# Decode attention and GLU block: four heads of one batch in a group, K in two halves of 32 KB rows, V as one tile of 64 KB rows

## The chip, the cores and the metric

One core of a Trainium2 chip. The experiments ran on three chips, each group beside runs of the kernel before on its own chip; the ratios are taken there. The metric is the device time of the kernel in microseconds (us), the median of several runs. "PE" is TensorE, "DVE" VectorE, "ACT" ScalarE, "POOL" GpSimd; "the transfer engines" are the core's 16 DMA engines.

A ratio is the mean time of one kernel's runs over the mean of the other's of the same rounds, so it is not quite the ratio of the medians that are quoted.

## The reference, cut to what matters

```python
# B=2, one query token, D=512, 32 heads of Dh=128, 8192 cached keys
q = (layernorm(x) @ wq)                                   # [2, 32, 128]
scores = einsum("bhqd,bhkd->bhqk", q, k_cache) * Dh**-0.5 # K: 134 MB
o = einsum("bhqk,bhkd->bhqd", softmax(scores), v_cache)   # V: 134 MB
h = x + o.reshape(2, 1, 4096) @ wo                        # wo: 4.2 MB
out = h + W_down(relu(gate(ln(h))) * up(ln(h)))           # F=1376, 4.2 MB
```

Every byte of K and V is read once: 268 of the 281 MB that the kernel reads.

## The kernel before

One unit of work is a pair of heads of one batch: 64 partitions for each head, 128 keys in each partition, so that a row is 128 x 128 x 2 bytes = 32 KB, for K and for V. Four slots of 4 MB hold K and V of two pairs in turn. The sync engine issues all loads.

```python
def kv(cache, p):
    hp, b = divmod(p, B)
    return cache[b, 2 * hp:2 * hp + 2].rearrange("h (p j) d -> (h p) (j d)", p=64)
def load(s, cache, p):
    nc.sync.dma_start(slot[s][:], kv(cache, p)).then_inc(slot_sem[s], 16)
```

DVE computes the scores of 96 of the 128 keys (a multiply with q, four halving adds and a reduction), PE those of the other 32 (transposes and matmuls). ACT takes the exponentials, one instruction per head and part; PE multiplies them with V. The loop over two pairs is a hardware loop on PE, DVE and ACT; POOL, SP and the tail are unrolled.

```python
with nc.Fori(0, NI, ...):                    # PE
    k_part(body, 0, ...)
    collect(body, 6)
    pv(body, 0, ...)
    k_part(body, 1, ...)
    o_gather(body)                           # the former outputs into one accumulator
    pv(body, 1, ...)
...
v_loads = [p] if p < NP - 5 else ...         # SP: slot of V is reloaded when its PV is done
for r in v_loads:
    sp.wait(tokp("pv", r))
    if r < NP - 3:
        load((2 * r + 1) % 4, A_v_cache, r + 2)
```

The whole text follows.

The softmax here doesn't subtract the row's maximum and nothing guards it: scores larger than these inputs give would overflow.

Of the kernel before, what the change touches and what calls it, by code (L numbers as in the profile page):

```python
# [39 lines left out]
def bass_sequential_preLN__gqa_block_cached__glu_gated_reglu__decode_kernel(  # L40
# [28 lines left out]
    DR = (H - 2) * Dh // 128  # L69
    NM = 6  # L70
# [5 lines left out]
    with ExitStack() as es:  # L76
# [14 lines left out]
        slot_sem = [S(f"slot{i}") for i in range(4)]  # L91
# [9 lines left out]
        slot = [sb(f"slot{i}", [128, SLOT], BF16) for i in range(4)]  # L101
        X = sb("X", [128, DR * D], BF16)
        wo_last = sb("wo_last", [128, 2 * D], BF16)
# [3 lines left out]
        QW = 8 + Dh  # L107
        q_all = sb("q_all", [128, NP, QW], BF16)
        qT = sb("qT", [128, NP * 2], BF16)
        q_c = [sb(f"q_c{i}", [128, QW], BF16) for i in range(2)]  # L110
# [5 lines left out]
        wo_rows, q_row = scr[:, 0:2 * D], scr[:, 2 * D:4 * D]  # L116
        pick = scr[:, 4 * D:5 * D].rearrange("p (s n) -> p s n", n=64)
        place = scr[:, 5 * D:6 * D].rearrange("p (h r d) -> p h r d", h=2, r=2)
# [9 lines left out]
        zs = sb("zs", [128, 4, 2], F32)  # L128
        zr = sb("zr", [128, 4], F32)
        zi = sb("zi", [128, 4], F32)  # L130
        O_cur = sb("O_cur", [128, 4], BF16)
        O_l = sb("O_l", [128, 2, B, 128], BF16)
        O_all = sb("O_all", [128, DR, B], BF16)
        mask = sb("mask", [128, DR // 2, NM], BF16)
        rows = sb("rows", [128, 2 * DR], BF16)
        rsel = sb("rsel", [128, 2, DR], BF16)
# [13 lines left out]
        zero = O_l[:, 0, 0, 0:B * DR]  # L150
# [8 lines left out]
        def kv(cache, p):  # L159
            hp, b = divmod(p, B)  # L160
            return cache[b, 2 * hp:2 * hp + 2].rearrange("h (p j) d -> (h p) (j d)", p=64)

        def tile(s):
            return slot[s][:].rearrange("p (j d) -> p j d", d=Dh)

        if True:

            def program():

                def load(s, cache, p):  # L170
                    nc.sync.dma_start(slot[s][:], kv(cache, p)).then_inc(slot_sem[s], 16)  # L171

                nc.scalar.dma_start(x_row, A_x[:, 0]).then_inc(sem_x, 16)
                nc.sync.dma_start(slot[3][:], A_wq.rearrange("(p c) n -> p (c n)", c=DC)).then_inc(sem_wq, 16)  # L174
                nc.sync.dma_start(  # L175
                    wo_rows, A_wo[128 * DR:].rearrange("(p r) n -> p (r n)", r=2)).then_inc(sem_wl, 16)
                load(0, A_k_cache, 0)
                load(1, A_v_cache, 0)
                load(2, A_k_cache, 1)


# [7 lines left out]
                for c in range(4):  # L189
                    pool.last()  # L190
                    pool.run(nc.gpsimd.tensor_copy(
                        out=sel[32 * c:32 * c + 32, :].rearrange("p (j q a) -> p j q a", j=VJ, q=PG),
                        in_=ident_f[32 * c:32 * c + 32, 32 * c:32 * c + 16].rearrange("p (q j a) -> p j q a", j=VJ, q=PG)))
# [6 lines left out]
                for sgn, base in ((1, 0), (-1, DR - 1)):  # L200
                    pool.last()
                    pool.run(nc.gpsimd.affine_select(
                        out=mask[:], in_=mask[:], pattern=[[2 * sgn, DR // 2], [-DR * sgn, NM]],
                        compare_op=ALU.is_ge, fill=0.0, base=base, channel_multiplier=sgn))
# [3 lines left out]
                for bank in Op:  # L208
# [4 lines left out]
                    in_=ident[:].rearrange("p (t r) -> p t r", r=32)[:, :, 0:B].unsqueeze(3).broadcast_to([128, 4, B, 64])))  # L213
                pool.run(nc.gpsimd.memset(place, 0.0))
                pool.last()
                for r in range(2):
                    t_place = pool.run(nc.gpsimd.tensor_copy(
                        out=place[:, :, r, r:128:2], in_=ident[:].rearrange("p (h i) -> p h i", h=2)))
# [31 lines left out]
                wq = slot[3][:].rearrange("p (c n) -> p c n", c=DC)  # L250
# [16 lines left out]
                for m in range(8):  # L267
# [5 lines left out]
                    out=qT[:].rearrange("p (t m b a) -> p t m b a", t=4, b=B, a=2),  # L273
                    in_=Wp[:].bitcast(BF16).rearrange("p (m a t r) -> p t m r a", m=4, a=2, t=4)[:, :, :, 0:B, :]))
                pe.wait(t_qT)
                for r in range(2):
                    for h in range(2):
                        i = nc.tensor.matmul(
                            Sp[r][64 * h:64 * h + 64, 0:2 * NP], lhsT=ident[:].rearrange("p (n r) -> p r n", r=2)[:, r, :],
                            rhs=qT[:], start=True, stop=True)  # L280
                t = pe.run(i)
                dve.run(nc.vector.memset(q_all[:, :, 0:8], 0.0))
                dve.wait(t)
                dve.last()
                for r in range(2):
                    for h in range(2):
                        t_q2 = dve.run(nc.vector.tensor_copy(
                            out=q_all[64 * h:64 * h + 64, :, 4 * r + 2 * h:4 * r + 2 * h + 2],
                            in_=Sp[r][64 * h:64 * h + 64, 0:2 * NP].rearrange("p (n a) -> p n a", a=2)))
# [8 lines left out]
                t_sel = dve.run(nc.vector.tensor_copy(out=rows[:, DR:], in_=rows[:, 0:DR]))  # L298
                sp.wait(t_q)
                load(3, A_v_cache, 1)  # L300
# [6 lines left out]
                for m in range(8):  # L307
                    if m >= 2:
                        pe.wait(t_cp[m - 2])
                    for a in range(2):  # L310
                        mm = nc.tensor.matmul(
                            Op[m % 2][64 * a:64 * a + 64, :], lhsT=pick[:, m, :],
                            rhs=q_row.rearrange("p (m a d) -> p m a d", a=2, d=Dh)[:, :, a, :], start=True, stop=True)
                    t_mm[m] = pe.run(mm)
                    act.wait(t_mm[m])
                    p0 = 8 * (m // B) + m % B
                    t_cp[m] = act.run(nc.scalar.activation(
                        out=q_all[:, p0:p0 + 7:2, 8:QW], in_=Op[m % 2][:].rearrange("p (k d) -> p k d", d=Dh),
                        func=ACT.Copy))
                t_q_b = t_cp[7]  # L320
                pe.wait((sem_wl, 16))
                for h in range(2):
                    for r in range(2):
                        mm = nc.tensor.matmul(
                            Tp[h][:], lhsT=place[:, h, r, :], rhs=wo_rows[:, r * D:(r + 1) * D], start=(r == 0), stop=(r == 1))
                    t = pe.run(mm)
                    act.wait(t)
                    t_wl = act.run(nc.scalar.activation(out=wo_last[:, h * D:(h + 1) * D], in_=Tp[h][:], func=ACT.Copy))
# [7 lines left out]
                nc.tensor.matmul(Ob[:, 0:ZC + 8], lhsT=onesn[:], rhs=ident[:, 0:ZC + 8], start=True, stop=True)  # L336
# [14 lines left out]
                def k_part(T, p, ev, k_wait):  # L351
                    s = (2 * p) % 4
                    k_t = tile(s)
# [3 lines left out]
                    def score(g):  # L357
                        wait(a2p, ev[g])
                        kv_ = kT[g % 2][:].rearrange("p (k n r) -> p k r n", n=128, r=2)
                        for k in range(GT // 2):  # L360
                            jj = g * GT + 2 * k
                            for r in range(2):
                                i = nc.tensor.matmul(  # L363
                                    Sp[p % 2][:, 2 * jj:2 * jj + 4], lhsT=kv_[:, k, r, :],
                                    rhs=q_c[p % 2][:, 4 * r:4 * r + 4], start=(r == 0), stop=(r == 1))
# [25 lines left out]
                def pv(T, p, parts, between=None):  # L391
                    s = (2 * p + 1) % 4
                    v_t = tile(s)
                    q = p % PG
                    n = 0
                    for j0, j1, waits in parts:
# [5 lines left out]
                        for j in range(j0, j1, VJ):  # L402
# [5 lines left out]
                            if T is body and n == 0:  # L408
# [4 lines left out]
                def collect(T, a):  # L413
                    nc.tensor.wait_ge(a2p, a)
                    for jj in range(VJ):
                        i = nc.tensor.matmul(  # L416
                            Ob[:, 0:4], lhsT=os_sb[:, jj * Dh:(jj + 1) * Dh],
                            rhs=sel[:, 4 * jj:4 * jj + 4], start=(jj == 0), stop=(jj == VJ - 1))
# [5 lines left out]
                def z_sum(bank):  # L424
                    return nc.tensor.matmul(bank[:, ZC:ZC + 8], lhsT=ones_f[:], rhs=zs[:], start=True, stop=True)  # L425

                def o_gather(T):
                    for a in range(2):
                        for b in range(B):
                            i = nc.tensor.matmul(  # L430
                                Op[1][:, b * DR:(b + 1) * DR], lhsT=O_l[:, a, b, :], rhs=rsel[:, a, :],
                                start=False, stop=False, skip_group_check=True)
                    T.mark("og", i)

                with nc.Fori(0, NI, engines=OrderedEngineSet([nc.tensor.engine])):
                    k_part(body, 0, (1, 2, 3, 4), ((k2p, 1),))
                    collect(body, 6)
                    pv(body, 0, ((JC, J, ((slot_sem[1], 16), (a2p, 5))), (0, JC, ((a2p, 7),))))
                    k_part(body, 1, (8, 9, 10, 11), ((k2p, 2),))
                    nc.tensor.wait_ge(l2p, 1)  # L440
                    o_gather(body)
                    nc.tensor.sem_inc(l2p, -1)
                    pv(body, 1, ((JC, J, ((slot_sem[3], 16), (a2p, 12))), (0, JC, ((a2p, EV),))))
                    z_sum(Ob)
                    nc.tensor.sem_inc(slot_sem[1], -16)
                    nc.tensor.sem_inc(slot_sem[3], -16)
# [11 lines left out]
                nc.tensor.wait_ge(l2p, 1)  # L458
                o_gather(tail)
# [7 lines left out]
                pv(tail, P0, ((JC, J, ((slot_sem[1], 16),)), (0, JC, ((a2p, 13),))))  # L467
# [14 lines left out]
                def tokp(kind, p, *g):  # L482
                    return tok(kind if kind == "og" else (kind, p) + g, p // 2)
# [5 lines left out]
                def exp(p, k, src):  # L489
                    q = p % PG  # L490
                    j0, j1 = ((JC, J), (0, JC))[k]
                    for a in range(2):
                        h = slice(64 * a, 64 * a + 64)
                        i = nc.scalar.activation(  # L494
                            out=e_t[q][h, j0 // VJ:j1 // VJ, 8 * q:8 * q + 8].rearrange(
                                "p g (j a) -> p g j a", a=2)[:, :, :, a],
                            in_=src(h, a), func=ACT.Exp, scale=inv_sqrt_dh,
                            accum_out=zs[h, 2 * q + a, k:k + 1])
# [357 lines left out]
```

## Time and profile before

| | before |
|---|---|
| time, median | 659.99 us (659.79 to 660.20, 6 runs) |
| span of the profiled run | 658.6 us |
| bytes read | 281.05 MB, 427 GB/s over the span |
| transfer packets | 10645 |
| DVE, PE, ACT, POOL busy | 469, 326, 214, 73 us |
| one turn of the loop (two K and two V loads) | 38.86 us |

How to read it: the profile counts an engine as busy while an instruction of it runs. No computing engine is near the span, and the row of slices for the transfer engines is full from end to end (0.9 or more in each of the 40 but the first and the last). The turn is the time from one multiply that waits for K to the next such multiply, in the chain that ended last: twelve turns between 131.15 and 597.46 us. The lines are in the prediction below.

### The profile page before, as it was taken

What the parts mean: (1) busy time and instruction counts of PE and PEld (TensorE: products, weight loads), DVE (VectorE), ACT (ScalarE), POOL (GpSimd) and SP (SyncE); (2) the same over time, 40 slices, a digit from 0 to 9 for tenths busy, and PEclk for the clock granted to TensorE, in tenths of its full rate; (3) what the DMA queues carried; (4) which work ended last, traced back from release to release, by engine and by line L of the source; (5) the groups of instructions that cost most, each with busy time, mean ns of one, the idle gap of its engine ahead of it and who ended that gap; (6) DMA issues with size and microseconds to landing.
All of it is one profiled execution on the core that took longest, in us unless ns stands there. A gap on an engine that the chain in (4) does not pass through costs nothing.

```text
span 658.6 us, 7569 instructions
## 1 busy us (share of the span) xinstructions
PE 326.1 (50%) x3066; PEld 192.1 (29%) x3067; DVE 469.4 (71%) x280; ACT 214.2 (33%) x433; POOL 72.7 (11%) x125
## 2 busy tenths in 40 slices
PE   2753444435554354644535453554445454454586
PEld 0431322214332132422213232322323222232354
DVE  1585576788767678776768867677876767787991
ACT  1622332243342233334223243323324322433151
POOL 3001002020200202020020201102020010202000
PEclk9999565565576555576655577555566755557567
DMA  8999999999999999999999999999999999999997
GB/s 366 445 426 437 426 442 418 442 420 444 424 436 438 422 440 420 444 422 438 430 432 438 422 440 420 444 422 438 440 422 436 424 438 424 440 428 436 434 415 307
DMA packets 10645, 281.17 MB, mean 427 GB/s; under 512 B 1190, under 2 KB 1292, under 8 KB 1804
## 3 DMA queue, kind: packets, MB, share of 16 engines
q1 hardware_dynamic: 10628, 281.06, 99.4%
q8 instruction: 5, 0.08, 0.0%
q14 instruction: 4, 0.03, 0.0%
q10 hardware_dynamic: 8, 0.00, 0.0%
HBM read 281.05 MB, written 0.00 MB: 427 GB/s over the span
## 4 chain that ended last, share of the span: by engine, by line
DMA 80%; DVE 18%; issue 1%; SPq 0%; DVEq 0%; PE 0%
DMA slot<-in_A_k_cache_dram 76%; DVE prod L539 16%; DMA slot<-in_B_W_down_dram 4%; DVE prod L548 2%; DVE scores L553 0%; SPq L171 0%; SPq L702 0%; SPq L698 0%; DVE kT L815 0%; DVEq L586 0%; PE O L807 0%; DVEq L590 0%; SPq L175 0%; SPq L174 0%; DVE zi L505 0%
## 5 line engine op out<-in xcount | busy, mean ns | idle before, releaser
L539 DVE TENSOR_TENSOR prod<-slot,q_c 128x12288 bf16<-128x12288 bf16 x32 | 209.9, 6558 | 148.1 <-DMA slot<-in_A_k_cache_dram 141.4
L404 PE MATMUL O<-slot,e 128*16 128x512 bf16 x1024 | 117.2, 609 | 219.3 <-ACT e L494 146.3
L548 DVE TENSOR_TENSOR prod<-prod 128x6144 bf16<-128x6144 bf16 (+3 forms) x128 | 212.3, 1658 | 7.8
L565 ACT ACTIVATE kT<-T 128x1024 bf16<-128x1024 bf16 x128 | 126.2, 1022 | 144.6 <-PE T L380 141.7
L380 PE MATMUL T<-ident_f,slot 128*128 128x128 f32 x512 | 112.8, 376 | 29.4 <-DVEq L586 29.4
L404 PEld LDWEIGHTS O<-slot,e 128*16 128x16 bf16 x1024 | 26.1, 112 | 284.6 <-ACT e L494 172.9
L494 ACT ACTIVATE e<-scores 64x96 bf16<-64x96 f32 x64 | 19.5, 304 | 239.8 <-DVEq L600 237.0
L380 PEld LDWEIGHTS T<-ident_f,slot 128*128 128x128 f32 x512 | 81.9, 193 | 44.4 <-DVEq L586 43.6
L536 POOL COPY q_c<-q_all 128x136 bf16<-128x136 bf16 x32 | 56.3, 1760 | 196.4 <-DVEq L590 152.5
L363 PE MATMUL S<-q_c,kT 128*128 128x4 bf16 x1024 | 47.6, 168 | 39.2 <-ACT kT L565 38.5
L363 PEld LDWEIGHTS S<-q_c,kT 128*128 128x128 bf16 x1024 | 39.6, 104 | 66.8 <-ACT kT L565 65.5
L416 PE MATMUL Ob<-sel,os_sb 128*128 128x4 f32 x136 | 31.0, 351 | 24.0 <-ACT os_sb L568 24.0
L416 PEld LDWEIGHTS Ob<-sel,os_sb 128*128 128x128 f32 x136 | 29.5, 319 | 25.9 <-ACT os_sb L568 25.9
L519 POOL MEMSET O_l<- 128x40 bf16 (+1 forms) x13 | 1.8, 136 | 303.9 <-DVEq L597 303.9
L553 DVE TENSOR_REDUCE scores<-prod 128x96 f32<-128x768 bf16 x32 | 30.5, 953 | 2.8
L565 ACT ACT_TABLE_LOAD x15 | 19.2, 1283 | 0.3
L494 ACT ACTIVATE e<-S 64x32 bf16<-64x32 f32 x64 | 13.0, 203 | 15.1 <-PE S L363 14.7
L568 ACT ACTIVATE os_sb<-O 128x512 f32<-128x512 f32 x17 | 10.2, 597 | 11.6 <-PE O L404 11.3
L494 ACT ACTIVATION_READ_ACCUMULATOR e<-S 64x1 f32 x64 | 12.8, 201 | 0.7
L494 ACT ACTIVATION_READ_ACCUMULATOR e<-scores 64x1 f32 x64 | 11.8, 184 | 0.0
L425 PEld LDWEIGHTS Ob<-zs,ones_f 128*128 128x128 f32 x30 | 7.1, 294 | 12.8 <-issue 12.8
L524 POOL COPY rsel<-rows 128x30 bf16<-128x30 bf16 x28 | 5.9, 209 | 33.3 <-DVEq L597 32.5
(104 smaller groups left out, 90.6 us busy)
## 6 DMA issues: line engine op xcount, KB each, us to landing
slot<-in_A_k_cache_dram SPq DMA_DIRECT2D x32, 4096.0 KB, 32.1
slot<-in_A_v_cache_dram SPq DMA_DIRECT2D x31, 4096.0 KB, 30.3
slot<-in_A_wq_dram SPq DMA_DIRECT2D x1, 4096.0 KB, 12.1
X<-in_A_wo_dram SPq DMA_DIRECT2D x1, 3840.0 KB, 46.0
slot<-in_A_v_cache_dram SPq DMA_DIRECT2D x1, 3072.0 KB, 23.1
slot<-in_B_W_up_dram SPq DMA_DIRECT2D x1, 1376.0 KB, 21.7
slot<-in_B_W_gate_dram SPq DMA_DIRECT2D x1, 1376.0 KB, 24.7
slot<-in_A_v_cache_dram SPq DMA_DIRECT2D x1, 1024.0 KB, 25.2
```

Of the source, the lines that this page charges most:

```text
L363: i = nc.tensor.matmul(Sp[p % 2][:, 2 * jj:2 * jj + 4], lhsT=kv_[:, k, r, :], rhs=q_c[p % 2][:, 4 * r:4 * r + 4], start=(r == 0), stop=(r ...
L380: i = nc.tensor.transpose(Tp[g % 2][:, k * 128:(k + 1) * 128], k_t[:, j:j + 2, :].rearrange("p j d -> p (j d)").bitcast(F32), ident_f[:])
L404: i = nc.tensor.matmul(Op[0][c:c + 16, :], lhsT=e_t[q][:, j // VJ, :], rhs=v_t[:, j:j + VJ, :].rearrange("p j d -> p (j d)"), start=(q == ...
L416: i = nc.tensor.matmul(Ob[:, 0:4], lhsT=os_sb[:, jj * Dh:(jj + 1) * Dh], rhs=sel[:, 4 * jj:4 * jj + 4], start=(jj == 0), stop=(jj == VJ - 1))
L425: return nc.tensor.matmul(bank[:, ZC:ZC + 8], lhsT=ones_f[:], rhs=zs[:], start=True, stop=True)
L494: i = nc.scalar.activation(out=e_t[q][h, j0 // VJ:j1 // VJ, 8 * q:8 * q + 8].rearrange("p g (j a) -> p g j a", a=2)[:, :, :, a], in_=src(h ...
L536: nc.gpsimd.tensor_copy(out=q_c[p % 2][:], in_=q_all[:, p]).then_inc(g2d, 1)
L539: return nc.vector.tensor_tensor(out=prod[:, 0:JC, :], in0=tile((2 * p) % 4)[:, 0:JC, :], in1=q_c[p % 2][:, 8:QW].unsqueeze(1).broadcast_t ...
L548: run(nc.vector.tensor_tensor(out=prod[:, 0:JC, 0:w], in0=prod[:, 0:JC, 0:w], in1=prod[:, 0:JC, w:2 * w], op=ALU.add))
L553: return nc.vector.tensor_reduce(out=scores[p % PG][:, 0:JC], in_=prod[:, 0:JC, 0:8], axis=AX.X, op=ALU.add)
L565: to_pe(nc.scalar.activation(out=kT[gg % 2][:], in_=Tp[gg % 2][:].bitcast(BF16), func=ACT.Copy))
L568: to_pe(nc.scalar.activation(out=os_sb[:], in_=Op[0][:], func=ACT.Copy))
```

## The change

A group is now four heads of one batch, 32 partitions each with 256 keys in a partition. K is loaded in two halves, so its rows stay at 32 KB and its two buffers at 4 MB, but the rows are now 64 KB apart in memory. V is one tile of 8 MB in rows of 64 KB, with one buffer. The intent is fewer and longer rows at the same total of on-chip memory. What follows from four heads: the exponentials take four instructions instead of two; q is copied once per group; the outputs gathered into the large wo product are those of 28 heads, and the last four heads get their own path.

```diff
-        slot = [sb(f"slot{i}", [128, SLOT], BF16) for i in range(4)]
+        K = [sb(f"K{i}", [128, SLOT], BF16) for i in range(2)]
+        V = sb("V", [128, 2 * SLOT], BF16)
...
+        def k_rows(p):
+            hq, b = divmod(p // 2, B)
+            return A_k_cache[b, A * hq:A * hq + A].rearrange(
+                "h (p k j) d -> k (h p) (j d)", p=128 // A, k=2)[p % 2]
+        def v_rows(o):
+            hq, b = divmod(o, B)
+            return A_v_cache[b, A * hq:A * hq + A].rearrange("h (p j) d -> (h p) (j d)", p=128 // A)
...
                     k_part(body, 0, (1, 2, 3, 4), ((k2p, 1),))
                     collect(body, 6)
-                    pv(body, 0, ...)
                     k_part(body, 1, (8, 9, 10, 11), ((k2p, 2),))
-                    nc.tensor.wait_ge(l2p, 1)
-                    o_gather(body)
-                    nc.tensor.sem_inc(l2p, -1)
-                    pv(body, 1, ...)
+                    pv(body, 0, ((JC, J, ((v_sem[0], 16),)), (0, JC, ())))
+                    pv(body, 1, ((JC, J, ((v_sem[1], 16), (a2p, 12))), (0, JC, ((a2p, EV),))))
                     z_sum(Ob)
+                    nc.tensor.wait_ge(l2p, 1)
+                    o_gather(body)
...
-                    for a in range(2):
-                        h = slice(64 * a, 64 * a + 64)
+                    for a in range(A):                       # A = 4
+                        h = slice(32 * a, 32 * a + 32)
                         i = nc.scalar.activation(...)        # exp
...
+                    if p % 2 == 1 and p < P0 - 3:            # SP: both PV passes done
+                        sp.wait(tokp("pv", p))
+                        load_v(p // 2 + 1, 0, 2 * J, v_sem[0])
```

The V tiles of the last two groups are loaded in pieces, so that their halves come free early.

## The prediction

> **What bounds the kernel now.** I read the page's slices and packet counts first, then the chain that ended last, then the stretch table of one loop turn, then the timeline of the tail.
>
> ```profile
> DMA  8999999999999999999999999999999999999997
> DMA packets 10645, 281.17 MB, mean 427 GB/s; under 512 B 1190, under 2 KB 1292, under 8 KB 1804
> slot<-in_A_k_cache_dram SPq DMA_DIRECT2D x32, 4096.0 KB, 32.1
> slot<-in_A_v_cache_dram SPq DMA_DIRECT2D x31, 4096.0 KB, 30.3
> ```
>
> The transfer engines are busy in all 40 slices; only the first and the last are lower. A 4 MB load lands 32.1 us after its issue, though one such load moves in under 10 us, so about three loads stand ahead of each one in the queue. 281.17 MB over the 658.6 us span is the 427 GB/s of the line.
>
> ```profile
> 98.94 32.09 DMA slot<-in_A_k_cache_dram
> ...
> 137.79 32.08 DMA slot<-in_A_k_cache_dram
> ...
> 170.00 6.57 DVE prod L539
> ...
> 629.40 26.68 DMA slot<-in_B_W_down_dram
> 656.09 0.04 issue
> 656.13 0.52 PE O L807 x7
> ```
>
> The chain runs from one K landing to the next: 98.94 + 32.09 = 131.03, and 137.79 + 32.08 = 169.87. One loop turn is 38.84 us. The 6.57 us of VectorE that the chain shows between landing and next issue is only when the next load is queued; it leaves no hole, because others stand in the queue. The end of the span is a landing too, that of W_down at 656.09.
>
> ```profile
> 131.10:169.95 38.85, 18.72 (x174) 10.80 (x174) 28.79 (x15) 12.85 (x26) 4.53 (x7) 0.58 1.00 432
> ```
>
> This is the stretch of one turn; the columns are length, then busy time of PE, PE weight loads, DVE, ACT and POOL, the granted clock, the DMA share and GB/s. DVE has 10 us spare in a turn, PE 20, ACT 26. DMA share is 1.00. So the body is bound by transfer alone, at 4 x 4.194 MB / 38.84 us = 432.0 GB/s.
>
> [...] The packet records of this trace agree with a fixed part: packets of 512, 1024, 4096, 8192 and 24576 bytes take 27, 46, 159, 309 to 313 and 912 ns; [...]so every packet pays some 8 to 9 ns[...]. [...] In this trace rows at pitches of 11, 30 and 32 KB all move at the full rate; a 64 KB pitch is not shown. [...] The records have five such 16384-byte packets on another queue, two of them at 32.5 and 57.6 us, and after each of those one transfer engine's completion marks stand about 1.5 us behind where they stood before, until the end.
>
> **The change part by part.**
>
> *Bytes.* None goes. wo is 3584 + 512 KB instead of 3840 + 256 KB. [...]
>
> *Packets.* A turn has now 4 loads x 128 rows / 16 engines = 32 packets of 32768 bytes for each engine. [...] After, a turn is two K halves (16 packets of 32 KB) and one V tile of 64 KB rows. If a 64 KB row is one packet, 8 pay the fixed part instead of 16. Fourteen of the sixteen V tiles are loaded so (groups 14 and 15 stay in pieces): 14 x 8 x 8.3 ns = 0.93 us. The V loads fall by 14, so 14 completion writes of 9 ns go: 0.13 us. wo: 8 packets of 4096 bytes at 159 ns and 8 of 28672 (about 1062) give 9.77 us for each engine, and before 8 x 84 and 8 x 1138 gave 9.78: nothing. Sum of this part: -1.06 us, all on the binding resource.
>
> *Does the queue stay full with one V tile?* This is the one structural danger: V has a single 8 MB buffer, which is refilled only when both PV passes are done. Let V land at t. By then both K halves (landed at t - 29.1 and t - 19.4) have been through VectorE, at 14.3 us each (6.56 + 6.7 + 0.95 and gaps): done by t - 0.4 or so. PV takes, by the rows below, 1.03 + 2.74 us for one half.
>
> ```profile
> 140.78 1.03 PE L404 MATMUL O<-slot,e 128*16 128x512 bf16 x8 [4.54 <-DMA slot<-in_A_v_cache_dram]
> ...
> 146.48 2.74 PE L404 MATMUL O<-slot,e 128*16 128x512 bf16 x24 [4.67 <-ACT e L494]
> ```
>
> Both halves are then done at about t + 8 and V is issued. The queue holds two K loads, which last until t + 19.4. That is some 11 us in hand. The K loads are issued when the multiply is through: at about t - 22 and t - 8, due at t and t + 9.7, so 22 and 18 us in hand. No hole in the steady turn.
>
> *The single q copy.* It waits for the first PV matmul of the group, so for V's landing at t, and takes 3.48 us at worst (POOL's row beside a busy DVE); K is multiplied from t + 9.7. About 6 us in hand, nothing on the path.
>
> *ScalarE.* The exponentials go from 2 to 4 instructions, each of the same free size: 4 x (0.20 + 0.20) and 4 x (0.30 + 0.19) per half instead of twice; a turn's exp time goes from 3.5 to 7.0 us, ACT from 12.9 to about 16.4 of 38.8. Off the path; before PV it adds about 1 us to t + 1, which is inside the 11 us.
>
> *POOL.* 16 q copies instead of 32, and fewer, wider spread operations; in the instruction listing 91 rows instead of 123. Off the path.
>
> *The tail.* The order becomes V14a, K30, V14b, K31, V15a, V15b in two parts, then 4.2 MB of FFN weights. K29 lands one load earlier than before relative to the end, K30, K31 and the last V pieces where they did. K31 lands 2 x 9.7 + 9.8, about 29 us, before the weights are in; VectorE, which is behind by one K half there now, has time to catch up: it finishes about 15 us before (now 13), then exp (2 us instead of 1). The projection of the last heads is 16 matmuls instead of 8:
>
> ```profile
> 648.82 0.43 PE L719 MATMUL W<-O_cur,wo_last 128*128 128x2 bf16 x8 [0.33 <-DVE O_cur L509]
> ...
> 652.68 1.72 PE L755 MATMUL O<-d_b,slot 128*128 128x2 bf16 x44 [0.45 <-DMA slot<-in_B_W_gate_dram]
> ...
> 656.13 0.38 PE L807 MATMUL O<-slot,hd 128*2 128x128 bf16 x8 [0.20 <-DMA slot<-in_B_W_down_dram]
> ```
>
> That is +0.4 us, and the gate matmuls waited 0.45 us for their weights, so it is just absorbed. 0 to +0.1.
>
> *The head.* More small matmuls and two more copies, +3 to 4 us before the first multiply (now at 26.8); the queue then holds K, V and wo until about 61 us, and the next K is due only then. Nothing.
>
> *Sum:* 659.83 - 1.06 + 0.05 = 658.8[...].
>
> **The rivals.** (a) *A 64 KB row is cut in two packets.* [...]no record here is larger than 32768 bytes, so this is open; a quarter. Then only the completions go: 659.7. (b) *V's single buffer leaves the transfer idle*, because PV is late or the clock falls. Then each of 14 turns gains a hole; a hole of 2 us makes 687, slower by 4%. Against it: 11 us in hand from measured durations. 3%. (c) *The new pitch (64 KB rows, four heads apart) costs rate.* 1% of rate would be 6.5 us: 665. [...] 5%. (d) *The instruction fetches fall on other engines.* [...]the completion marks of the last loads are up to 1.85 us apart, mostly by the two early fetches. If two fall on one engine +1.4 us, if none falls on a late one -1.4. This moves the time as much as the change itself: 657.3 to 660.2. (e) *The doubled exp or the projection shows at the end*: at most +1 us.
>
> **Range and chances.** The centre is 658.7. (d) gives about 1.4 either way, (a) and (e) up to +1, (c) a thin tail above: 657.2 to 660.9. Faster by over 2% would need 646.6[...]: 0.01. Slower by over 2% is (b) and part of (c): 0.03. The rest, 0.96, is within 2%.
>
> **What would show it.** Packets should fall from 10645 by 14 x 128 + 14 x 16 = 2016, to about 8630; if rows are cut, only to about 10420. A turn should be 38.77 us by the chain, DMA share 1.00 in its stretch, the chain still mostly K landings, ACT some 57 us busier (the four exp rows of the page, 19.5 + 13.0 + 12.8 + 11.8, doubled), DVE unchanged near 469. The last landing should still be W_down. I would be wrong if a slice in the middle shows the DMA below 9, if the chain names V loads that wait for PV with few loads in the queue, if a turn is longer than 38.9, or if the last release is not a landing.

The sum came to 658.8 us; a last term of 0.1 us, for a late instruction packet that shorter programs might spare, is cut, and with it the forecast was the 658.7 that follows. The 8.3 ns for a packet are the author's estimate. The records of the trace before bear it out: two packets of 512 bytes take 2 x 27 ns and one of 1024 takes 46, two of 2048 take 2 x 84 and one of 4096 takes 159, six of 4096 take 6 x 159 and one of 24576 takes 912, so each packet more cost 8, 9 and 8.4 ns. What the idea could gain at most can be estimated from the same figures: 10645 packets at 8 to 9 ns, over 16 engines, are 5.3 to 6.0 us in all, and 2% would be 13.2. The rows at pitches of 11, 30 and 32 KB are the packets of 11008, 30720 and 32768 bytes, with medians of 418, 1140 and 1218 ns, 26 to 27 bytes in each ns. The five packets of 16384 bytes are those of the page's line "q8 instruction"; in that trace the 16 completion marks of the K or V load that landed at 23 us lie within 0.4 us, in the loads from 32.7 to 52.1 us one mark stands 1.8 to 1.9 us behind the first, and from 61 us on two do. That the end would move with them by 1.4 us was an estimate from these marks, and no run shows it.

## The result, and the profile after

| | before | after |
|---|---|---|
| time, median of 6 runs | 659.99 us | 658.91 us (658.77 to 659.48) |
| ratio | | 0.9985 (0.9972 to 0.9998): the same at 2% |
| span of the profiled run | 658.6 us | 657.5 us |
| one turn | 38.86 us | 38.78 us |
| transfer packets | 10645 | 8629 |
| DVE, PE, ACT, POOL busy | 469, 326, 214, 73 us | 469, 307, 274, 25.5 us |

The time fell by 1.08 us. First the page's slices and packets, and from the list of transfers the V loads:

```profile
DMA  9999999999999999999999999999999999999997
DMA packets 8629, 281.17 MB, mean 428 GB/s; under 512 B 966, under 2 KB 1068, under 8 KB 1580
...
V<-in_A_v_cache_dram SPq DMA_DIRECT2D x3, 4096.0 KB, 31.7
...
V<-in_A_v_cache_dram SPq DMA_DIRECT2D x14, 33.2
```

The transfers are still busy from end to end. There are 2016 packets fewer with the same bytes, which is 14 x 128 rows that are one packet instead of two, and 14 x 16 completion writes. The 14 lines at the bottom are the whole V tiles. The packet records show 1792 packets of 65536 bytes with a median of 2422 ns, where two of 32768 take 2 x 1218.

Then the chain that ended last (start, length, what), in the loop and at the end:

```profile
118.45 32.02 DMA K<-in_A_k_cache_dram
...
157.23 32.01 DMA K<-in_A_k_cache_dram
...
625.15 26.62 DMA K<-in_B_W_gate_dram
651.77 0.05 issue
651.82 1.74 PE O L775 x44
...
653.90 1.12 PE O L827 x32
```

118.45 + 32.02 = 150.47 and 157.23 + 32.01 = 189.24: a turn of 38.77. Over the twelve turns from 111.81 to 577.17, by the multiplies, the mean is 38.780 against 38.859 before. At the end the chain now goes over the landing of the gate weights and PE's work on them, not over W_down.

Third, a stretch of one turn (length, then busy time of PE, PE weight loads, DVE, ACT and POOL, the granted clock, DMA share, GB/s), and the timeline of PV in that turn:

```profile
200.00:238.80 38.80, 17.55 (x174) 12.26 (x174) 28.81 (x16) 16.71 (x42) 1.02 (x5) 0.59 1.00 432
```

```profile
218.36 4.91 PE L428 MATMUL O<-V,e 128*16 128x512 bf16 x64 [6.94 <-DMA V<-in_A_v_cache_dram]
219.02 0.30 POOL L560 COPY q_c<-q_all 128x144 bf16<-128x144 bf16 x1 [14.64 <-PE O L428]
...
223.31 0.33 SPq L189 DMA_DIRECT2D V<-in_A_v_cache_dram  x1
```

The same two lines of an earlier turn (timeline from 130 to 150 us):

```profile
140.80 6.13 PE L428 MATMUL O<-V,e 128*16 128x512 bf16 x64 [6.95 <-DMA V<-in_A_v_cache_dram]
...
146.98 0.33 SPq L189 DMA_DIRECT2D V<-in_A_v_cache_dram  x1
```

The DMA share is 1.00 although V has one buffer. PE waits for V, does both passes in 4.9 us in the first turn shown, which has the shortest of all, and in 6.1 us in the other; over the 14 turns it is 4.9 to 6.5 us, at a mean granted clock of 0.73 to 0.55. V's next load is issued as soon as they are done. In the first turn the last K load ahead of it in the queue is in at 235.2 us on the first engine to finish it. The q copy, which waits for the same landing, takes 0.30 us.

Last, the rows of ScalarE's exponentials (name and shape, count, busy us and mean ns, idle before): the first two lines are from the page before, the last two from the page after.

```profile
L494 ACT ACTIVATE e<-scores 64x96 bf16<-64x96 f32 x64 | 19.5, 304 | 239.8 <-DVEq L600 237.0
L494 ACT ACTIVATE e<-S 64x32 bf16<-64x32 f32 x64 | 13.0, 203 | 15.1 <-PE S L363 14.7
```

```profile
L517 ACT ACTIVATE e<-scores 32x96 bf16<-32x96 f32 x128 | 53.9, 421 | 196.5 <-DVEq L625 193.3
L517 ACT ACTIVATE e<-S 32x32 bf16<-32x32 f32 x128 | 29.8, 233 | 16.1 <-PE S L388 15.0
```

Half the partitions for each instruction saved nothing here. The records of 96 columns went from 304 to 421 ns, but these overlap with the instruction behind them (lines of the timelines, first before and then after):

```profile
360.08 0.31 ACT L494 ACTIVATE e<-scores 64x96 bf16<-64x96 f32 x1 [7.57 <-DVEq L600]
360.27 0.19 ACT L494 ACTIVATION_READ_ACCUMULATOR e<-scores 64x1 f32 x1
360.47 0.30 ACT L494 ACTIVATE e<-scores 64x96 bf16<-64x96 f32 x1
```

```profile
359.73 0.42 ACT L517 ACTIVATE e<-scores 32x96 bf16<-32x96 f32 x1 [6.60 <-DVEq L625]
359.92 0.23 ACT L517 ACTIVATION_READ_ACCUMULATOR e<-scores 32x1 f32 x1
360.16 0.42 ACT L517 ACTIVATE e<-scores 32x96 bf16<-32x96 f32 x1
```

From one exponential of 96 columns to the next it is 387 ns before and 437 after (medians), so each costs 50 ns more, not 117. ACT as a whole is 60 us busier, and none of it shows in the turn.

### The profile page after: what moved, and what is told of

It reads as the page before. It is cut to its first block, busy times and chain, and to the rows that moved or that the text cites. A ratio compares the mean times of both kernels' runs of the same rounds, so it can differ in the third digit from the quotient of the medians.

```text
span 657.5 us, 7820 instructions
## 1 busy us (share of the span) xinstructions
PE 306.7 (47%) x3096; PEld 202.9 (31%) x3097; DVE 469.1 (71%) x275; ACT 274.0 (42%) x687; POOL 25.5 (4%) x96
## 2 busy tenths in 40 slices
DMA packets 8629, 281.17 MB, mean 428 GB/s; under 512 B 966, under 2 KB 1068, under 8 KB 1580
## 4 chain that ended last, share of the span: by engine, by line
DMA 80%; DVE 15%; PE 3%; issue 1%; ACT 0%; DVEq 0%; SPq 0%
DMA K<-in_A_k_cache_dram 69%; DVE prod L563 15%; DMA V<-in_A_v_cache_dram 5%; DMA K<-in_B_W_gate_dram 4%; DMA V<-in_A_wq_dram 2%; PE T L345 1%; PE O L428 1%; PE O L272 1%; ACT kT L589 0%; PE O L775 0%; PE O L827 0%; PE O L330 0%; PE Ob L440 0%; PE T L405 0%; DVE prod L281 0%
## 5 line engine op out<-in xcount | busy, mean ns | idle before, releaser
L563 DVE TENSOR_TENSOR prod<-K,q_c 128x12288 bf16<-128x12288 bf16 x32 | 209.9, 6558 | 146.7 <-DMA K<-in_A_k_cache_dram 136.0
L405 PE MATMUL T<-ident_f,K 128*128 128x128 f32 x512 | 123.3, 403 | 134.6 <-DVEq L611 134.6
L428 PE MATMUL O<-V,e 128*16 128x512 bf16 x1024 | 91.4, 533 | 111.8 <-DMA V<-in_A_v_cache_dram 111.8
L517 ACT ACTIVATE e<-scores 32x96 bf16<-32x96 f32 x128 | 53.9, 421 | 196.5 <-DVEq L625 193.3
L405 PEld LDWEIGHTS T<-ident_f,K 128*128 128x128 f32 x512 | 88.6, 206 | 137.6 <-DVEq L611 137.5
L428 PEld LDWEIGHTS O<-V,e 128*16 128x16 bf16 x1024 | 30.5, 117 | 165.3 <-DMA V<-in_A_v_cache_dram 113.3
L388 PE MATMUL S<-q_c,kT 128*128 128x8 bf16 x1024 | 48.6, 171 | 44.8 <-ACT kT L589 44.6
L517 ACT ACTIVATE e<-S 32x32 bf16<-32x32 f32 x128 | 29.8, 233 | 16.1 <-PE S L388 15.0
L517 ACT ACTIVATION_READ_ACCUMULATOR e<-scores 32x1 f32 x128 | 30.0, 235 | 0.0
L517 ACT ACTIVATION_READ_ACCUMULATOR e<-S 32x1 f32 x128 | 25.6, 200 | 1.5
## 6 DMA issues: line engine op xcount, KB each, us to landing
V<-in_A_wq_dram SPq DMA_DIRECT2D x1, 4096.0 KB, 12.3
```

The lines of the kernel that those rows point to most:

```text
L388: i = nc.tensor.matmul(Sp[p % 2][:, A * jj:A * jj + 2 * A], lhsT=kv_[:, k, r, :], rhs=q_c[:, 2 * A * r:2 * A * r + 2 * A], start=(r == 0), ...
L405: i = nc.tensor.transpose(Tp[g % 2][:, k * 128:(k + 1) * 128], k_t[:, j:j + 2, :].rearrange("p j d -> p (j d)").bitcast(F32), ident_f[:])
L428: i = nc.tensor.matmul(Op[0][c:c + 16, :], lhsT=e_t[q][:, j // VJ, :], rhs=v_t[:, j:j + VJ, :].rearrange("p j d -> p (j d)"), start=(q == ...
L517: i = nc.scalar.activation(out=e_t[q][h, j0 // VJ:j1 // VJ, :].rearrange("p g (j a) -> p g j a", a=A)[:, :, :, a], in_=src(h, a), func=ACT ...
L563: return nc.vector.tensor_tensor(out=prod[:, 0:JC, :], in0=tile(K[p % 2], p)[:, 0:JC, :], in1=q_c[:, Q2:QW].unsqueeze(1).broadcast_to([128 ...
```

## The experiments

All are edits of the changed kernel. The theory: the gain is the fixed part of each packet and each completion write that is no longer there, on an otherwise full transfer queue; everything else lies beside it. The rivals: the gain comes from the shorter programs, the regrouping or a luckier end; or the single V buffer and the doubled exponentials take some of it back.

### Control

The changed kernel unaltered, on the chip of the next three runs.

> The changed kernel again, as the control on this chip beside the runs below. Both theories: 658.9, about 1.1 under the kernel before, 8629 packets.

Measured: 658.89 us (5 runs) against 659.78 before (9 runs), ratio 0.9984 (0.9971 to 0.9998), 8629 packets. As expected, so the difference of 1 us is seen again on another occasion.

### V in rows of 32 KB again, all else kept

```diff
-                        load_v(p // 2 + 1, 0, 2 * J, v_sem[0])
+                        load_v(p // 2 + 1, 0, J, v_sem[0])
+                        load_v(p // 2 + 1, J, 2 * J, v_sem[1])
```

(and the same for the first tile; each half has its own completion; the semaphore that stood for the second half is no longer set beforehand)

> The changed kernel with V loaded as two transfers of 32 KB rows, issued one behind the other, all else kept. Theory (the gain is the fixed 8.3 ns of each packet and 9 ns of each completion write): 14 x 8 packets and 14 completions per engine come back, +0.93 +0.13 us, 660.0, 10645 packets as before the change, a turn of 38.85 to 38.86 us. Rival (the gain comes from the shorter POOL and SP programs, the regrouping or a luckier drain at the end): it keeps 658.9 and a turn of 38.78.

Measured: 659.79 us (659.60 to 660.22, 5 runs), ratio to the kernel before 0.9999 (0.9985 to 1.0012). Its packet line and two links of its chain:

```profile
DMA packets 10645, 281.17 MB, mean 427 GB/s; under 512 B 1190, under 2 KB 1292, under 8 KB 1804
```

```profile
118.61 32.09 DMA K<-in_A_k_cache_dram
...
157.47 32.10 DMA K<-in_A_k_cache_dram
```

The packet line is that of the kernel before to the last figure. The twelve turns from 111.97 to 578.27 have a mean of 38.858, as before the change. Row length, with the one completion write more that each second load brings, gives and takes the whole gain: the shorter POOL and SP programs, the single q copy, the four heads and the new order of the tail are all still in this kernel and are worth nothing that these runs resolve. Against the control it is +0.90 us where 1.06 were expected.

### Many short packets in the same number of transfers

```diff
-        V = sb("V", [128, 2 * SLOT], BF16)
+        V = sb("V", [128, 8 * (32 * Dh + 16)], BF16)      # 32 bytes of padding after each 8 KB
+        Vb = V[:].rearrange("p (n w) -> p n w", n=8)
...
-                    nc.sync.dma_start(V[:, k0 * Dh:k1 * Dh], v_rows(o)[:, k0 * Dh:k1 * Dh]).then_inc(sem, 16)
+                    dst = Vb[:, k0 // 32:k1 // 32, 0:32 * Dh]
+                    nc.sync.dma_start(dst, v_rows(o)[:, k0 * Dh:k1 * Dh].rearrange("p (n w) -> p n w", w=32 * Dh)).then_inc(sem, 16)
```

> The changed kernel with the V tile padded by 32 bytes after every 8 KB, so that each V and wq transfer writes runs of 8 KB, with the number of transfers kept. Theory: 896 more packets per engine (14 x 56, and 112 for groups 14, 15 and wq) at 8.3 ns: +7.4 us, 666.3, about 22965 packets, no change of the completions. Rival (the fixed part of a packet is hidden when packets are queued, and the gain came from elsewhere): under +1 us.

Measured: 666.42 us (666.11 to 666.64, 4 runs), ratio 1.0100 (1.0085 to 1.0115).

```profile
DMA packets 22965, 281.17 MB, mean 423 GB/s; under 512 B 966, under 2 KB 1068, under 8 KB 1580
```

The diff is cut: the load of wq and the reads of V by PE follow the padded tile. The packets are as counted, and the time is 7.53 us above the control: 7530 / 896 = 8.4 ns for each packet. The turn is 39.229 (twelve from 113.02 to 583.77), 449 ns above that of the changed kernel for 56 packets, so 8.0 ns each. The fixed part was not hidden by the full queue here. For 32 against 64 KB rows the turns above (38.858 and 38.780) give 78 ns for 8 packets and one completion, so 8.7 each: about the same.

### Many short packets in many transfers

```diff
+                    n = 4 if sem in v_sem else 1
+                    w = (k1 - k0) * Dh // n
+                    for x in range(k0 * Dh, k1 * Dh, w):
+                        nc.sync.dma_start(V[:, x:x + w], v_rows(o)[:, x:x + w]).then_inc(sem, 16)
```

> The changed kernel with each V half loaded as four transfers of 8 KB rows. Theory: 856 more packets (+7.1 us) and 107 more completion writes (+0.96 us) per engine: 667.0, about 24040 packets. If a completion cost much more than its 9 ns record, say 0.1 us of an engine, it would be near 677; if issuing them held the queue back, the DMA share would fall below 1.00 in a turn.

(cut: V is loaded as two halves, and the waits count four transfers)

Measured: 667.21 us (666.68 to 667.52, 4 runs), ratio 1.0109 (1.0094 to 1.0125).

```profile
DMA packets 24037, 281.18 MB, mean 422 GB/s; under 512 B 2678, under 2 KB 2780, under 8 KB 3292
```

The turn is 39.314 (twelve from 112.58 to 584.35). Against the run before it has 7 completions more in a turn and the same packets: 85 / 7 = 12 ns each, near the 9 ns of the record. So a further transfer on the full queue cost 12 ns of an engine here, where the run before has 8.0 to 8.4 ns for each packet.

### V issued later: how much the single buffer has in hand

```diff
                     if p % 2 == 1 and p < P0 - 3:
-                        sp.wait(tokp("pv", p))
+                        sp.wait(tokp("pv", p), tokp("kf", p + 1))
```

> The changed kernel with each V load held back further: besides the two PV passes it waits for the last transposes of the next K half. In the trace of the changed kernel V is issued some 5 us after V landed and the queue lasts to 19.4 us after it; this moves the issue to about 13.5 us. Theory (the single V buffer costs nothing while it is issued before the queue runs out): 658.9, DMA share 1.00. Rival (the single buffer already costs something, or a shallower queue does): slower by 1 us or more.

Measured: 659.57 us (659.31 to 659.72, 5 runs), ratio to the kernel before 0.9995 (0.9982 to 1.0009); 0.7 above the changed kernel's median, and 0.6 to 0.7 above the two harmless changes below (exponentials, instruction block) on the same chip. Neither expectation holds: it is not 658.9 and not a microsecond. One turn in its timeline:

```profile
111.63 6.56 DVE L563 TENSOR_TENSOR prod<-K,q_c 128x12288 bf16<-128x12288 bf16 x1 [8.94 <-DMA K<-in_A_k_cache_dram]
...
116.08 0.33 SPq L189 DMA_DIRECT2D V<-in_A_v_cache_dram  x1
```

The turn stays 38.78 (twelve from 111.63 to 576.96), and the slowest of the 16 transfer engines is no later either: its completion mark of the load near 625 us stands at 625.0, as in the control of this kernel below. But the packet records show that other engines ran out of work: the first of them had its last K packet in at 118.9 us, 2.8 us after the issue. From 10 to 640 us the 16 engines together were idle for 2.0 us more than in the traces before and after the change (which have 1.1 us each in short gaps), near 118, 158 and 196 us. That alone is little, 0.13 us for each engine. The rest is in V's own packets: the 1792 of them take together 7.6 us longer than in the changed kernel, single ones 3.4 us instead of 2.4. Together it is 9.6 us of 16 engines, or 0.6 us each, and the mean completion mark near the end is 0.4 to 0.5 us later.

V was issued 2.3 to 3.1 us before the first engine was through with the K ahead of it. In the changed kernel it is 10.4 to 11.9 us (V is issued at 107.12 and the K ahead of it is in at 118.9), and no loss is seen. So an issue 2.3 to 3.1 us before that lost 0.6 us of each engine in all, and one 10.4 us or more before it lost nothing that is seen; where between them the loss stops, no run shows.

### V issued later still

```diff
-                        sp.wait(tokp("pv", p))
+                        sp.wait(tokp("pv", p), tokp("kf", p + 2))
```

> The same held back further still, until the second next K half is transposed, about 28.5 us after V landed, when the queue has been empty since 19.4. Theory: a hole of some 9 us[...] in each of the 13 turns concerned, a turn near 50 instead of 38.8 us, about 800 us in all, chain with V landings in it. It shows where the edge of the 14 us in hand is. Rival (there was no such edge near): no change.

Measured: 838.09 us, one run. A turn is 52.40 us; its stretch:

```profile
283.25:335.65 52.40, 16.83 (x175) 11.55 (x175) 28.79 (x15) 16.65 (x42) 1.09 (x5) 0.58 0.75 320
```

The DMA share falls to 0.75. 13 turns x (52.40 - 38.78) = 177 us, which with 658.9 makes 836. Size and sign are as the theory has them; the hole was 2 us longer than expected. (The 50 us expected for a turn were 38.8, the 9 of the hole and a term of 2 us.) After an issue on the empty queue V's first packet started 0.96 us later in this run, on the last engine at most 1.9. So the single buffer cost 13.6 us in a turn here, with V issued only after the queue had run empty.

### Every exponential twice

```diff
                         h = slice(32 * a, 32 * a + 32)
+                        nc.scalar.activation(out=e_scr[h, 2 * q + k, 0:j1 - j0]..., in_=src(h, a), func=ACT.Exp,
+                            scale=inv_sqrt_dh, accum_out=z_scr[h, 2 * q + k, a:a + 1])
```

> The changed kernel with every exponential done twice, the second time into a scratch tile: 8 instead of 4 activations for each part, about 110 us more ScalarE busy. Theory (the added exponentials lie beside the transfers): body unchanged, at most +0.5 us at the tail, 658.9 to 659.4. Rival (ScalarE's doubled work took back part of the gain): +1 us or more, a second time.

Measured: 658.86 us (658.62 to 660.41, 5 runs; three of them at most 658.86). ACT is busy for 324 instead of 274 us, less than the 110 more that were expected; in the timeline, instructions back to back overlap in part. The turn is 38.78. In the loop, ScalarE's part of the change is beside the transfers. At the tail it is less sure: two of the five runs, 659.75 and 660.41, are higher than every run of the changed kernel (659.48 at most), and the ratio to the kernel before, 0.9993 (0.9979 to 1.0007), does not tell it from either kernel. Whether that is the longer ACT chain at the tail or chance is open.

### One more block of instructions for PE

```diff
+                pe.wait(t_ident)
+                for n in range(128):
+                    nc.tensor.transpose(Wp[:].bitcast(BF16)[:, (n % 8) * 128:(n % 8) * 128 + 128], ident[:], ident[:])
                 pe.wait(t_ident, (sem_x, 16), t_ln)
```

> The changed kernel with 128 unused transposes at the start of PE's program, which waits there for wq anyway[...]. Theory (an instruction fetch puts one transfer engine behind by about 1.5 us, and the slowest engine sets the end): one more 16384-byte packet in the first 60 us, one more engine 1.5 us late in the completion marks; 658.9 if it is another engine, 660.4 if it is the late one. Rival (fetches do not matter for the spread of the engines): marks and time as in the changed kernel.

Measured: 658.99 us (658.54 to 659.36, 5 runs). One packet of 16384 bytes more, at 12.3 us, 8630 in all, with 256 instructions more on the page (8076 for the 7820 of the changed kernel). The completion marks of one load on the 16 engines, in ns after the first of them (packet records of the second control below, and of this run):

```text
control, 526 us: 0 24 47 131 151 164 177 185 186 208 261 274 497 767 1646 1906
this,    526 us: 0 68 106 119 130 237 238 322 329 364 366 460 759 1545 1629 1703
```

Three engines instead of two stand 1.5 us or more behind. So with one such packet more, at 12.3 us, one transfer engine more stood behind, and still did at 526 us. The time did not change; it was a third engine and not one of the two late ones, but whether that is the reason is not shown, nor that the slowest engine sets the end. That two fetches on one engine would cost 1.4 us was not seen in any run.

### The two runs that the late V left open, and a try to beat both kernels

The 0.7 us of the first late-V run might have been PE's tail at a low clock. So it was run again, with the changed kernel beside it, and both were run with the tail's wo product of 28 heads moved ahead of the last K half on PE.

```diff
                 k_part(tail, P0, (2, 3, 4, 5), ((k2p, 1),))
-                k_part(tail, P1, (7, 8, 9, 10), ((k2p, 2),))
-                nc.tensor.wait_ge(a2p, 12)
+                nc.tensor.wait_ge(a2p, 7)
                 ...                                         # 28 matmuls of wo
+                k_part(tail, P1, (8, 9, 10, 11), ((k2p, 2),))
```

(cut: on ACT, the copy of the 28 heads' outputs that this product reads also moves ahead of the last K half)

> The changed kernel as the control for the three runs below: 658.9.

Measured: 658.85 us (658.57 to 659.13, 5 runs), before 659.96 in 9 runs; ratio 0.9982 (0.9969 to 0.9996).

> The kernel with V held back for one K half, again. Its first run was 0.7 us above the changed kernel although its turn was the same 38.78; the difference began in the tail, where its granted PE clock was 0.50 against 0.79 and 0.72 and PE's chain, not a transfer, ended last. Theory (a chance of the granted clock in the tail): anywhere between 658.7 and 659.7, and in a run of the changed kernel's length the clock of the tail is higher. Rival (the later V issue itself costs): 659.5 again, in every run.

Measured: 659.56 us (659.30 to 661.14, 5 runs). The rival holds: the cost comes again. In the control's profiled run (659.13 us, the slowest of its five) PE also ran at a granted clock of 0.50 from 600 to 640 us, and no landing is in its chain after 640 us, so the low clock at the tail is not special to this kernel. What is special lies in the transfers: 4.2 us of idle more than in the control's trace and 7.4 us more for V's packets, together 0.7 us for each engine. And the weights at the end land later, whatever PE's clock. The third W_down load, in the control and then in this run (KB, us from issue to landing):

```profile
K<-in_B_W_down_dram SPq DMA_DIRECT2D x1, 256.0 KB, 26.5
```

```profile
K<-in_B_W_down_dram SPq DMA_DIRECT2D x1, 256.0 KB, 27.2
```

It is in at 655.71 us here, at 655.58 in the first late-V run and at 655.55 in the next run. In the six traces with V issued at its usual time (after, both controls, the doubled exponentials, the added block, the last run) it is in between 654.68 and 655.15.

> The same with the tail's wo product of 28 heads moved before the last K half on PE, which takes its 3 us out of the chain that PE ran at the low clock at the end. Theory (the 0.7 us are PE's chain in the tail): 658.9 or less, last release a landing. Rival (they come from the later V issue in the transfers): 659.5 stays.

Measured: 662.20 us (660.19 to 663.30, 5 runs), ratio 1.0040 (1.0027 to 1.0054). Neither expectation holds: the move has a cost of its own, as the next run shows, so this run does not decide between them.

> The changed kernel with only that move, as a candidate to beat it. Theory (in its usual runs a landing ends the chain with about 1.3 us of PE in hand): the same 658.8 to 658.9, with fewer runs above 659.1. Rival (PE's tail limits it too): 658.3.

Measured: 661.53 us (660.08 to 661.97, 5 runs), ratio 1.0018 (1.0004 to 1.0032): slower than both kernels. The longest wait of PE from 636 to 650 us, by the waits of the changed kernel and then of this one (for whom: us in all, times, longest):

```profile
PE O L428 <- DMA V<-in_A_v_cache_dram: 2.1, 2, 1.3
```

```profile
PE O L428 <- ACT e L517: 3.1, 1, 3.1
```

The move made the last K half 5 us later on PE than in that trace, and 4 us later than in the control's (its first transposes at 631.7 instead of 626.0 and 627.8). ACT's program has the evacuations of that half before the exponentials of the half before, so these came late too, and PE waited for them where it had waited for V. A piece of 3 us was taken out of one place and a wait of 3 us on ACT took it over. That is why nothing was gained. It does not explain all of the 2.7 us that were lost: after the wait PE itself was slower, with 24 matmuls on V in 2.67 us where the control took 1.40, at a granted clock of 0.60 from 640 to 652 us against 0.92. Why the clock was lower no run shows. No version was found that beats the changed kernel.

## Why the prediction was right

The predicted 658.7 us was measured as 658.91, inside the range. The prediction started from 659.83 us, so its gain was 1.13 us, of which 1.06 are packets and completions; the measured gain, from 659.99, is 1.08. The last 0.1 us did not come: there are five packets of 16384 bytes in both traces.

*Bytes.* Held: DMA share 1.00, and between 10 and 640 us the 16 transfer engines together were idle for 1.1 us in either trace.

*Packets.* Held, and this step is shown, not argued. The count was 8629 for "about 8630"; the turn 38.780 for 38.77. Restoring the packets restores the time (38.858 and 659.79), and multiplying them costs 8.0 to 8.4 ns each, for 8.3 in the prediction. Rival (a), a row cut in two, is excluded by the 1792 records of 65536 bytes.

*The queue with one V tile.* Held, but two terms were mis-sized. PV of both halves takes 4.9 to 6.5 us, not the 7.5 of the rows before; the granted clock was 0.50 in those rows and is 0.55 to 0.73 now, but no run singles it out as the reason. So V is issued 5 to 7 us after landing and not 8. And I took an issue as in time if it came before the queue ended. In the first late-V run an issue 2.3 to 3.1 us earlier still lost 0.6 us for each engine; the transfer engines are up to 2 us apart (1906 ns in the marks of the second control), and in the run held back further the first packet started 0.96 us after an issue. Measured on the first engine to finish, 10.4 to 11.9 us lie between issue and the queue's end; less the 3 that were too few, some 7 to 9 are left (an estimate from these numbers), where I had said 11.

*Pitch*, rival (c). Excluded: K rows 64 KB apart take the same median of 1218 ns as before.

*ScalarE.* Held in sum (60 us for 57 predicted), though its term was wrong twice. I had added up records that overlap (0.30 + 0.19 us, where one exponential of 96 columns follows another after 0.387), and I had taken "the same free size" to mean the same time, where the step went to 0.437 us. The two errors go opposite ways, so the sum is in part luck. Why the step grew, no run shows. Off the path in the loop, by the run with doubled exponentials.

*The single q copy.* 0.30 us in every turn and 3.00 for the last group, instead of 3.48 at worst. Off the path as said.

*The head.* I expected the first multiply 3 to 4 us later; it is at 26.40 instead of 26.79. For q, 32 small matmuls and 4 evacuations replaced 16 and 8. In the traces of the other runs with this change it is between 24.8 and 28.0 us, so a shift of 3 to 4 us did not come. No effect on the end, as said.

*The tail.* "The last landing should still be W_down" did not hold for the chain: it names the gate weights, with PE's work after them; W_down's third load is in at 655.01 us, 0.01 before PE comes to its last matmuls. In the first control's profile the last release is W_down, and in the second control's there is no landing at all after 640 us, at a clock of 0.50. A last release that is no landing was on the list of signs of being wrong, and here it came true. The projection's 16 matmuls take 0.69 instead of 0.43 us. The tail is closer to a tie between PE and the transfers than the prediction said, within the fractions of a microsecond that it allowed.

*Rival (d), the fetches.* The two early packets of 16384 bytes moved (from 32.5 and 57.6 to 24.9 and 58.6 us) and still left two engines late, 1.7 and 2.1 us behind the first in the marks near 70 us. With the added block a third stood 1.5 us behind; a change of the end by 1.4 us did not occur. That the span ends with the slowest of the 16 engines was the assumption and is not borne out: in the late-V runs the slowest engine's marks stayed where they were (625.0 us), and the last weights landed later, with the mean of the marks (0.4 to 0.5 us).

What stays open is why the tail's granted clock differs from run to run (0.50 to 0.79 between 615 and 628 us), and whether the spread of a few tenths of a microsecond, or of 2 us where work is moved in the tail, goes with it.

## What to carry to other kernels

When the transfer queue never runs dry, count packets: from the measured turn of 38.84 us, 8.3 ns for each packet and 9 for the completion that go on each engine gave this kernel's turn to 0.01 us (38.77 for 38.780), and all 10645 packets at that price are 5.5 us, an estimate by which the change could not be worth 2%, 13.2 us. Larger tiles cost buffers, and whether that matters here is one subtraction, the time from the issue to the end of what is queued ahead: 10.4 us or more of it cost nothing that is seen, 2.3 to 3.1 us cost 0.6 us for each engine, and an issue on the empty queue cost 13.6 us a turn. Work that was moved off PE's chain in the tail was not saved: ACT, whose program has its own order, then came later, and PE waited 3.1 us for it.
